# Opening weights in 512-byte rows on one queue, and a first wave by pairs of rows

## The chip, the cores and the metric

The kernel runs on one core of one Trainium2 chip. The metric is the device time of one execution in microseconds (us). Times come from plain executions; the views come from one profiled execution, whose own time is given beside its span.

## The reference

A layer norm over the last axis without scale and shift, a matrix product with a bias and a tanh-approximated gelu, and a second matrix product with a bias. All inputs and the output are bf16.

```python
B, S, D, F = 1, 2048, 1024, 3584

def reference(x, w1, b1, w2, b2):
    y = _layernorm(x, axis=-1)                               # eps 1e-5
    h = _gelu(jnp.einsum("bsd,df->bsf", y, w1) + b1)          # w1: D x F
    return jnp.einsum("bsf,fd->bsd", h, w2) + b2              # w2: F x D
```

## The kernel before

**Tiling.** The 2,048 tokens are four blocks of 512 (`TB`), each of four tiles of 128 tokens. The contraction over D = 1,024 has eight blocks of 128, called dt (`DT`). The F = 3,584 hidden columns are 28 row blocks of 128, called r (`FT`). The first product computes, for row r, a [128 hidden x 512 tokens] piece in one PSUM bank from eight matmuls, one for each dt; ScalarE applies the gelu with the bias and writes `hT_sb`. The second product takes 28 matmuls for each [128 tokens x 512 columns] piece of the output; VectorE adds b2 and SyncE stores. All weights stay in SBUF.

**How the order is made.** Each engine has its own program, a list filled by the Python code and emitted at the end. The order within an engine is the order in which the lines are appended; a wait sits in front of the operation that has it, and everything behind it on that engine waits too. Signals between engines are semaphores; each DMA has a semaphore of its own, which counts sixteen parts, one from each of the sixteen DMA engines.

**The opening, which the change touches.** The first block can't wait for its layer norm, so its four tiles go three ways.

- Tiles 0 and 1 (`RAW`) are multiplied raw, without mean and scale. `pe_T(0, ...)` and `pe_T(1, ...)` transpose them on TensorE, ScalarE copies them to `yT_sb` (line 353). Statistics go on the side, and the result is repaired in PSUM: `ops_fix` adds the mean times the column sum of the weights and multiplies by the scale (lines 512 and 515), then comes the gelu. For the later rows (r of 7 and up) the transposed tiles are centred in place, `ops_centre` (line 505), and only the scale is applied in PSUM (line 420). The centring overwrites what the first wave reads, so it waits for the wave's last matmul (`wave01`).
- Tiles 2 and 3 are normalised by VectorE (`op_stats` line 250, `op_aggr` line 260 with a power on GpSimd at line 257, `ops_norm` line 264) and then transposed on TensorE; these transposes are called T2 and T3.
- The first seven rows (`R_WAVE`) run as waves over seven PSUM banks, cell by cell, all at line 394. A cell is one matmul: row r, contraction block dt. The first wave, over tiles 0 and 1, has 56 cells of 258 columns (two of them hold ones, which give the column sums). Then tile 2 has 56 cells of 128 columns, in the order halves of dt, rows, dt in the half. Then tile 3 has 56 cells, row by row. From row 7 on, `mm1_row` takes all four tiles at once (line 381).

The first wave runs dt by dt: all seven rows for dt 0, then all seven for dt 1. Its weights come in the same way, one transfer for each dt with the columns of all seven rows (896 columns, 1,792 bytes per row of w1). T2 stands ahead of dt 6 (`T2_BEFORE`), T3 after 14 cells of tile 2's wave (`T3_AT`).

**The queues.** SyncE (SP) issues x0, x1, w0, w2, x2, w4, w5, x3, w6, w7 and then the rest: the other columns of w1 (640, 1,024 and 1,024 wide, all eight dt in one transfer), x for the second block, w2 in four parts, b2, the rest of x. ScalarE (ACT) issues b1, w1 and w3, where w1 and w3 are here the transfers of dt 1 and dt 3. All are made at line 187.

**VectorE's order in the opening** (line 521): the statistics of tiles 0 and 1; the bias operations `ops_b1` (lines 490 and 493), which turn b1 into a column for each row; the statistics of tile 2; the first half of `ops_row_turn` (line 479), which turns the statistics of the raw tiles into rows; the norm of tile 2; the statistics of tile 3; the second half of the turn; the norm of tile 3; `ops_row_spread` (line 484), which copies those rows to all partitions; the two centrings; then the fixes.

Of the kernel before, what the change touches and what calls it, by code (L numbers as in the profile page):

```python
# [12 lines left out]
P = 128  # L13
TB = 512
TPB = TB // P
# [5 lines left out]
RAW = (0, 1)  # L21
# [2 lines left out]
GROUPS_0 = (0, 4, 8)  # L24
GROUPS_1 = (0, 8)
HALVES = (0, 4, 8)
T2_BEFORE = 6
T3_AT = 14
W1_COLS = (640, 1024, 1024)
N_W2_CHUNKS = 4  # L30
SP_FIRST_LOADS = ("x0", "x1", "w0", "w2", "x2", "w4", "w5", "x3", "w6", "w7")
ACT_FIRST_LOADS = ("b1", "w1", "w3")
SLOT_0 = (1, 2, 3, 0)
N_ONES = 2

# [56 lines left out]
def bass_standalone__mixer_channel_mlp__prompt_kernel(  # L92
# [13 lines left out]
    DT = D // P  # L106
# [7 lines left out]
    R = R_WAVE  # L114
    assert R == NB1 + NB2 and R < FT
    assert NB1 + NB2 + 1 <= 8 and NB2 == 2
    assert all(c[-1] == DT for c in (GROUPS_0, GROUPS_1, HALVES))
    assert T2_BEFORE < DT and TPB == 4 and RAW == (0, 1)

    w1_chunks = [(j, j + 1, 0, R * P) for j in range(DT)]  # L120
    c0 = R * P
    for wdt in W1_COLS:
        w1_chunks.append((0, DT, c0, c0 + wdt))
        c0 += wdt
# [17 lines left out]
    with ExitStack() as es:  # L142
# [67 lines left out]
        def issue(item):  # L210
            if item == "b1":
                dma(b1r_sb[0:FT, :], b1.rearrange("(t p) -> t p", p=P), "b1", F * 2, waits=["b1z"])
            elif item[0] == "x":
                load_x_tile(int(item[1:]))
            elif item[0] == "w" and int(item[1:]) < len(w1_chunks):
                load_w1(int(item[1:]))

        act.op(lambda e: e.preload_act_table(ACT.Gelu_apprx_tanh))
        dma_q[0] = act
        for item in ACT_FIRST_LOADS:  # L220
            issue(item)
        dma_q[0] = sp
        for item in SP_FIRST_LOADS:
            issue(item)
# [18 lines left out]
        for i in range(NT):  # L243
            n = 6 * parts(i)
# [3 lines left out]
        def op_stats(i, h):  # L248
            pw = D // parts(i)
            return (lambda e, i=i, h=h, pw=pw: e.bn_stats(st_sb[i][:, 6 * h:6 * (h + 1)],  # L250
                                                          x_sb[:, i, h * pw:(h + 1) * pw]),
                    [x_ev[i][h if len(x_ev[i]) == parts(i) else 0]], f"st{i}_{h}", 0.03 + pw * 0.0012)

        def op_aggr(i):
            mv = stat_r[:, i, 0:2] if i in RAW else mv_sb[:, i, :]
            dst = stat_r[:, i, 2:3] if i in RAW else rstd_sb[:, i:i + 1]
            pool.op(lambda e, i=i, dst=dst, mv=mv: e.tensor_tensor(out=dst, in0=mv[:, 1:2], in1=nhalf[:, i:i + 1],  # L257
                                                                   op=ALU.pow),
                    waits=[f"mv{i}", "nhalf"], sig=f"rstd{i}")
            return (lambda e, i=i, mv=mv: e.bn_aggr(mv, st_sb[i][:, :]),  # L260
                    [f"st{i}_{parts(i) - 1}", f"eps{i}"], f"mv{i}", 0.33)
# [9 lines left out]
        def ops_norm(i):  # L271
            cuts = (0, DT)
            y_ev[i] = []
            res = []
            for k, (j0, j1) in enumerate(zip(cuts[:-1], cuts[1:])):
                res.append(op_norm(i, j0 * P, j1 * P, f"y{i}_{k}"))
                y_ev[i] += [f"y{i}_{k}"] * (j1 - j0)
            return res
# [84 lines left out]
        def new_unit():  # L363
            u = unit_n[0]
            unit_n[0] += 1
            bank = first_ring[u] if u < len(first_ring) else ("1", (u - len(first_ring)) % NB1)
            waits = [bank_gelu[bank]] if bank in bank_gelu else []
            name = f"{bank[0]}_{bank[1]}"
            if not waits and name in bank_read:
                waits.append(bank_read[name])  # L370
            return bank, waits
# [16 lines left out]
        def pe_wave(r, dt, tiles, bank, waits, sig):  # L388
            n0 = slot(tiles[0]) * P - (N_ONES if tiles[0] == 0 else 0)
            n1 = (slot(tiles[-1]) + 1) * P  # L390
            w = list(waits) + [f"w1c{w1_chunk_of(r, dt)}"] + [yT_ev[t][dt] for t in tiles]
            if tiles[0] == 0:
                w.append("onecols")
            pe.op(lambda e: e.matmul(  # L394
                unit_bank(bank)[:, n0:n1], lhsT=w1_sb[:, dt, r * P:(r + 1) * P], rhs=yT_sb[:, 0, dt, n0:n1],
                start=(dt == 0 and tiles[0] in (0, 3)), stop=(dt == DT - 1), skip_group_check=True),
                waits=w, sig=sig)
            pe_t[0] += _mm_us(n1 - n0)
            if sig:
                est[sig] = pe_t[0]  # L400
# [73 lines left out]
        def ops_row_turn():  # L474
            res = []
            for tq in range(4):
                src = flat[32 * tq:32 * (tq + 1), :, :].to_broadcast([32, 4, 32])
                dst = row_r[0:32, :, 32 * tq:32 * (tq + 1)]
                res.append((lambda e, src=src, dst=dst: e.transpose(out=dst, in_=src), ["rstd0", "rstd1"],
                            ("row_q" if tq == 3 else None), 0.31))  # L480
            return res

        def ops_row_spread():
            return [(lambda e, q=q: e.tensor_copy(out=row_r[32 * q:32 * (q + 1), :, :], in_=row_r[0:32, :, :]),
                     ["row_q"], ("row_r" if q == 3 else None), 0.35) for q in range(1, 4)]

        def ops_b1():
            res = []
            for q in range(4):
                res.append((lambda e, q=q: e.transpose(out=b1t_sb[32 * q:32 * (q + 1), :],  # L490
                                                       in_=b1r_sb[:, 32 * q:32 * (q + 1)]),
                            ["b1", "b1z"], ("b1t" if q == 3 else None), 0.2))
            res.append((lambda e: e.tensor_copy(out=b1_sb[:, :], in_=b1t_sb[:, 0:FT]), ["b1t"], "b1c", 0.18))
            return res
# [5 lines left out]
        def ops_centre():  # L500
            res = []
            for t in RAW:
                xt = yT_sb[:, 0, :, slot(t) * P:(slot(t) + 1) * P]
                m = row_r[:, 2 * t, :].unsqueeze(1).to_broadcast([P, DT, P])
                res.append((lambda e, xt=xt, m=m: e.tensor_tensor(out=xt, in0=xt, in1=m, op=ALU.subtract),  # L505
                            ["row_r", "wave01"], f"ctr{t}", 1.23))
            return res
# [10 lines left out]
        st = {i: [op_stats(i, 0), op_stats(i, 1), op_aggr(i)] for i in range(TPB)}  # L518
        nm = {i: ops_norm(i) for i in (2, 3)}
        turn = ops_row_turn()  # L520
        seq = st[0][:2] + st[1][:2] + [st[0][2], st[1][2]] + ops_b1()
        seq += st[2] + turn[:2] + nm[2] + st[3] + turn[2:] + nm[3] + ops_row_spread() + ops_centre()
        for o in seq:
            dve_put(o)

# [3 lines left out]
        wave = [new_unit() for _ in range(R)]  # L529
        opened = set()  # L530

        def wave_cell(r, dt, tiles, sig=None):
            waits = [] if r in opened else wave[r][1]
            opened.add(r)
            pe_wave(r, dt, tiles, wave[r][0], waits, sig)

        early = [r for r in range(R) if not wave[r][1]] + sorted((r for r in range(R) if wave[r][1]),
                                                                 key=lambda r: wave[r][1])
        for dt in range(DT):
            if dt == T2_BEFORE:  # L540
                pe_T(2, GROUPS_1, ("t",))
            for k, r in enumerate(early):
                wave_cell(r, dt, RAW, "wave01" if dt == DT - 1 and k == R - 1 else None)
        n = 0
        for j0, j1 in zip(HALVES[:-1], HALVES[1:]):
            for r in range(R):
                for dt in range(j0, j1):
                    if n == T3_AT:
                        pe_T(3, GROUPS_1, ("t",))
# [25 lines left out]
        for b in range(NB):  # L575
# [11 lines left out]
            for st in range(TPB):  # L587
                for dh in range(DH):
                    c0, c1 = dh * NCH, (dh + 1) * NCH
# [72 lines left out]
```

## Time and profile before

| | before |
|---|---|
| runs | 399.11, 399.95, 398.2 us |
| median | 399.11 us |
| profiled execution, its own time | 399.24 us |
| its span | 397.8 us |
| PE busy | 392.0 us (99%) |
| DVE busy | 155.1 us (39%) |
| ACT busy | 81.0 us (20%) |
| weights of the opening (224 KB each) from SP, issue to landing | 6.5 us median of six |
| x tiles of 256 KB, issue to landing | 4.9 us median of four |
| granted TensorE clock | 1.0 |

PE is TensorE, PEld its weight loads, DVE is VectorE, ACT is ScalarE, POOL is GpSimd and SP is SyncE. A busy PE in this table means that matmuls were in flight. Times inside the execution count from the start of the span. The chain of waits is the work that ended last, followed back from the last instruction to what released it.

### The profile page before, as it was taken

The numbers are of one execution on the slowest core, as the hardware profiler recorded it, in microseconds if no ns is written. First come the engines' busy times: TensorE is split into PE (matmuls) and PEld (weight loads), VectorE is DVE, ScalarE is ACT, GpSimd is POOL, SyncE is SP. The second block draws the span as 40 slices with busy tenths as digits, with TensorE's granted clock in tenths as the row PEclk, the third lists the DMA queues.
The fourth block names the chain that finished last, engine by engine and source line by source line (L and its number), as shares of the span: only waits on it lengthen the run. The fifth ranks groups of instructions, "written<-read, shape, count | busy, mean of one in ns | idle before, by whom it ended". The sixth has DMA issues, their size and how long they took to land.

```text
span 397.8 us, 4722 instructions
## 1 busy us (share of the span) xinstructions
PE 392.0 (99%) x2017; PEld 190.9 (48%) x2052; DVE 155.1 (39%) x338; ACT 81.0 (20%) x121; POOL 10.6 (3%) x56
## 2 busy tenths in 40 slices
PE   7999999999999999999999999999999999999998
PEld 7954444444444444444444444444444444444447
DVE  4968898989999004988100000001100000001011
ACT  2163430000034432000024334100003334400000
POOL 2101000010001000000000000000000000000000
PEclk9999999999999999999999999999999999999999
DMA  7999930000000000000000000000000000000001
GB/s 254 384 386 387 387 134 15 26 25 17 26 1 2 0 0 2 26 14 28 26 15 0 0 2 0 7 21 26 13 28 13 2 0 0 2 13 26 15 26 28
DMA packets 15326, 23.64 MB, mean 59 GB/s; under 512 B 1482, under 2 KB 7498, under 8 KB 15306
## 3 DMA queue, kind: packets, MB, share of 16 engines
q1 hardware_dynamic: 14976, 22.88, 16.1%
q10 hardware_dynamic: 330, 0.47, 0.4%
q8 instruction: 16, 0.26, 0.3%
q14 instruction: 4, 0.03, 0.0%
HBM read 19.14 MB, written 4.19 MB: 59 GB/s over the span
## 4 chain that ended last, share of the span: by engine, by line
PE 97%; DMA 1%; issue 1%; SPq 0%; DVE 0%
PE ps L446 48%; PE ps L381 45%; PE ps L394 3%; DMA w_sb<-in_w_dram 1%; PE ps_t L337 0%; SPq L187 0%; DVE o_sb L457 0%
## 5 line engine op out<-in xcount | busy, mean ns | idle before, releaser
L446 PE MATMUL ps<-w_sb,hT_sb 128*128 128x512 bf16 (+1 forms) x964 | 193.4, 360 | 0.8
L381 PE MATMUL ps<-yT_sb,w_sb 128*128 128x512 bf16 x821 | 180.8, 379 | 1.0
L446 PEld LDWEIGHTS ps<-w_sb,hT_sb 128*128 128x128 bf16 x980 | 91.3, 98 | 102.7
L381 PEld LDWEIGHTS ps<-yT_sb,w_sb 128*128 128x128 bf16 x840 | 82.2, 98 | 98.9
L404 ACT ACTIVATE hT_sb<-ps,b_sb 128x512 bf16<-128x512 f32 x112 | 76.7, 687 | 253.2 <-PE ps L381 231.8
L457 DVE TENSOR_TENSOR o_sb<-ps,b_sb 128x512 bf16<-128x512 f32 (+1 forms) x35 | 22.6, 646 | 198.9 <-PE ps L446 198.9
L307 DVE STREAM_TRANSPOSE yT_sb<-x_sb 32x256 bf16<-32x256 bf16 x192 | 83.7, 436 | 26.4 <-PE ps L381 23.3
L250 DVE BATCH_NORM_STATS2 st_sb<-x_sb 128x6 f32<-128x512 bf16 x32 | 20.9, 670 | 8.6 <-DMA x_sb<-in_x_dram 8.5
L394 PE MATMUL ps<-yT_sb,w_sb 128*128 128x128 bf16 (+1 forms) x168 | 12.9, 237 | 1.4 <-DMA w_sb<-in_w_dram 1.4
L394 PEld LDWEIGHTS ps<-yT_sb,w_sb 128*128 128x128 bf16 x168 | 11.7, 98 | 2.3 <-DMA w_sb<-in_w_dram 1.6
L257 POOL TENSOR_TENSOR rstd_sb<-mv_sb,nhalf 128x1 f32<-128x1 f32 x14 | 7.7, 548 | 115.3 <-DVE mv_sb L260 115.3
L420 DVE TENSOR_TENSOR ps<-ps,row_r 128x256 f32<-128x256 f32 x21 | 8.8, 426 | 3.9 <-PE ps L381 3.7
L264 DVE TENSOR_SCALAR x_sb<-x_sb,mv_sb,rstd_sb 128x1024 bf16<-128x1024 bf16 x14 | 7.6, 544 | 2.5 <-POOL rstd_sb L257 1.8
L468 PE MATMUL ps<-const-bfloat16-1.0 128*128 128x128 bf16 x32 | 3.8, 310 | 0.8 <-PEq L647 0.8
L353 ACT COPY yT_sb<-ps_t 128x512 int32<-128x512 int32 (+1 forms) x3 | 1.5, 514 | 11.4 <-PE ps_t L337 11.4
L468 PEld LDWEIGHTS ps<-const-bfloat16-1.0 128*128 128x128 bf16 x32 | 3.4, 144 | 0.8 <-issue 0.8
L512 DVE SCALAR_TENSOR_TENSOR ps<-row_r,ncs,ps 128x256 f32<-128x256 f32 x7 | 3.3, 478 | 0.0
L260 DVE BATCH_NORM_AGGREGATE mv_sb<-st_sb 128x2 f32<-128x15 f32 x14 | 3.1, 221 | 0.4
L515 DVE TENSOR_TENSOR ps<-ps,row_r 128x256 f32<-128x256 f32 x7 | 3.0, 432 | 0.2
L505 DVE TENSOR_TENSOR yT_sb<-yT_sb,row_r 128x1024 bf16<-128x1024 bf16 x2 | 2.4, 1222 | 0.0
L337 PE MATMUL ps_t<-ident,x_sb 128*128 128x128 bf16 x20 | 1.8, 236 | 0.0
L337 PE MATMUL ps<-ident,x_sb 128*128 128x128 bf16 x12 | 1.5, 311 | 0.0
(21 smaller groups left out, 13.4 us busy)
## 6 DMA issues: line engine op xcount, KB each, us to landing
w_sb<-in_w_dram SPq DMA_DIRECT2D x4, 1792.0 KB, 18.9
w_sb<-in_w_dram SPq DMA_DIRECT2D x2, 2048.0 KB, 17.3
out_dram<-o_sb SPq DMA_DIRECT2D x31, 128.0 KB, 1.7
x_sb<-in_x_dram SPq DMA_DIRECT2D x3, 1024.0 KB, 14.0
w_sb<-in_w_dram SPq DMA_DIRECT2D x6, 224.0 KB, 6.5
w_sb<-in_w_dram SPq DMA_DIRECT2D x1, 1280.0 KB, 10.3
x_sb<-in_x_dram SPq DMA_DIRECT2D x4, 256.0 KB, 4.9
w_sb<-in_w_dram ACTq DMA_DIRECT2D x2, 224.0 KB, 6.2
```

The costliest lines, as they stand in the source:

```text
L250: return (lambda e, i=i, h=h, pw=pw: e.bn_stats(st_sb[i][:, 6 * h:6 * (h + 1)], x_sb[:, i, h * pw:(h + 1) * pw]), [x_ev[i][h if len(x_ev[i ...
L257: pool.op(lambda e, i=i, dst=dst, mv=mv: e.tensor_tensor(out=dst, in0=mv[:, 1:2], in1=nhalf[:, i:i + 1], op=ALU.pow), waits=[f"mv{i}", "nh ...
L264: return (lambda e, i=i, c0=c0, c1=c1: e.tensor_scalar(out=x_sb[:, i, c0:c1], in0=x_sb[:, i, c0:c1], scalar1=mv_sb[:, i, 0:1], scalar2=rst ...
L307: res.append((lambda e, src=src, dst=dst: e.transpose(out=dst, in_=src), waits, (f"tr{i}" if lastop else None), 0.47))
L337: pe.op(lambda e, i=i, j=j, o=off, bap=bank_of[bname]: e.transpose(out=bap[:, o:o + P], in_=x_sb[:, i, j * P:(j + 1) * P], identity=ident[ ...
L381: pe.op(lambda e, b=b, r=r, dt=dt, bank=bank: e.matmul(unit_bank(bank)[:, 0:TB], lhsT=w1_sb[:, dt, r * P:(r + 1) * P], rhs=yT_sb[:, b % 2, ...
L394: pe.op(lambda e: e.matmul(unit_bank(bank)[:, n0:n1], lhsT=w1_sb[:, dt, r * P:(r + 1) * P], rhs=yT_sb[:, 0, dt, n0:n1], start=(dt == 0 and ...
L404: act.op(lambda e, r=r, n0=n0, n1=n1, bank=bank: e.activation(out=hT_sb[:, r, n0:n1], in_=unit_bank(bank)[:, n0:n1], func=ACT.Gelu_apprx_tanh,
L420: crit.append((est[sig], (lambda e, reg=reg: e.tensor_tensor(out=reg, in0=reg, in1=row_b(1), op=ALU.mult), [sig, "row_r"], ready, 0.45), 0))
L446: pe.op(lambda e, sl=sl, ft=ft, c0=c0, c1=c1, bank=bank: e.matmul(ps_2[:, bank, 0:c1 - c0], lhsT=hT_sb[:, ft, sl * P:(sl + 1) * P], rhs=w2 ...
L457: crit.append((est[sig], (lambda e, ob=ob, c0=c0, c1=c1, bank=bank: e.tensor_tensor(out=o_sb[:, ob, c0:c1], in0=ps_2[:, bank, 0:c1 - c0], ...
L468: pe.op(lambda e: e.matmul(ps_1[:, 0, 0:P], lhsT=ones, rhs=ones, start=True, stop=True))
```

## The change

The opening weights are cut another way. Instead of eight transfers of one contraction block each, with 896 columns (128 rows of 1,792 bytes), there are eight of four contraction blocks each, with 256 columns (512 rows of 512 bytes): the columns of two rows r, dt 0 to 3 in one transfer and dt 4 to 7 in the next. They hold eight rows r (1,024 columns), so that the next transfer has 512 columns in place of 640. All eight go on SyncE's queue, in order, with x2 after the first two and x3 after the sixth; ScalarE issues b1 alone.

The first wave follows: by pairs of rows (0,1), (2,3), (4,5) and then row 6, in each pair the first half of dt for its rows, then the second half. T2 now stands ahead of cell 40, which is the second half of the pair (4,5); T3 stands after 28 cells of tile 2's wave, which are all rows' first halves.

VectorE's order changes as well. The bias operations move from ahead of tile 2's statistics to behind the row spread; tile 3's statistics move behind them; the first centring moves ahead of tile 3's norm.

```diff
@@ -24,12 +24,15 @@
 GROUPS_0 = (0, 4, 8)
 GROUPS_1 = (0, 8)
 HALVES = (0, 4, 8)
-T2_BEFORE = 6
-T3_AT = 14
-W1_COLS = (640, 1024, 1024)
+PAIRS = ((0, 1), (2, 3), (4, 5), (6,))
+T2_AT = 40
+T3_AT = 28
+W1_EARLY = 4
+W1_EARLY_COLS = 256
+W1_COLS = (512, 1024, 1024)
 N_W2_CHUNKS = 4
-SP_FIRST_LOADS = ("x0", "x1", "w0", "w2", "x2", "w4", "w5", "x3", "w6", "w7")
-ACT_FIRST_LOADS = ("b1", "w1", "w3")
+SP_FIRST_LOADS = ("x0", "x1", "w0", "w1", "x2", "w2", "w3", "w4", "w5", "x3", "w6", "w7")
+ACT_FIRST_LOADS = ("b1",)
 SLOT_0 = (1, 2, 3, 0)
 N_ONES = 2
 
@@ -115,10 +118,11 @@
     assert R == NB1 + NB2 and R < FT
     assert NB1 + NB2 + 1 <= 8 and NB2 == 2
     assert all(c[-1] == DT for c in (GROUPS_0, GROUPS_1, HALVES))
-    assert T2_BEFORE < DT and TPB == 4 and RAW == (0, 1)
-
-    w1_chunks = [(j, j + 1, 0, R * P) for j in range(DT)]
-    c0 = R * P
+    assert TPB == 4 and RAW == (0, 1) and sum(PAIRS, ()) == tuple(range(R))
+
+    w1_chunks = [(j0, j1, k * W1_EARLY_COLS, (k + 1) * W1_EARLY_COLS) for k in range(W1_EARLY)
+                 for j0, j1 in zip(HALVES[:-1], HALVES[1:])]
+    c0 = W1_EARLY * W1_EARLY_COLS
     for wdt in W1_COLS:
         w1_chunks.append((0, DT, c0, c0 + wdt))
         c0 += wdt
@@ -518,8 +522,9 @@
         st = {i: [op_stats(i, 0), op_stats(i, 1), op_aggr(i)] for i in range(TPB)}
         nm = {i: ops_norm(i) for i in (2, 3)}
         turn = ops_row_turn()
-        seq = st[0][:2] + st[1][:2] + [st[0][2], st[1][2]] + ops_b1()
-        seq += st[2] + turn[:2] + nm[2] + st[3] + turn[2:] + nm[3] + ops_row_spread() + ops_centre()
+        ctr = ops_centre()
+        seq = st[0][:2] + st[1][:2] + [st[0][2], st[1][2]] + st[2] + turn[:2] + nm[2] + turn[2:] + ops_row_spread()
+        seq += ops_b1() + st[3] + ctr[:1] + nm[3] + ctr[1:]
         for o in seq:
             dve_put(o)
 
@@ -534,13 +539,12 @@
             opened.add(r)
             pe_wave(r, dt, tiles, wave[r][0], waits, sig)
 
-        early = [r for r in range(R) if not wave[r][1]] + sorted((r for r in range(R) if wave[r][1]),
-                                                                 key=lambda r: wave[r][1])
-        for dt in range(DT):
-            if dt == T2_BEFORE:
+        cells = [(r, dt) for rows in PAIRS for j0, j1 in zip(HALVES[:-1], HALVES[1:])
+                 for r in rows for dt in range(j0, j1)]
+        for n, (r, dt) in enumerate(cells):
+            if n == T2_AT:
                 pe_T(2, GROUPS_1, ("t",))
-            for k, r in enumerate(early):
-                wave_cell(r, dt, RAW, "wave01" if dt == DT - 1 and k == R - 1 else None)
+            wave_cell(r, dt, RAW, "wave01" if n == len(cells) - 1 else None)
         n = 0
         for j0, j1 in zip(HALVES[:-1], HALVES[1:]):
             for r in range(R):
```

## The prediction

> **What bounds the kernel now.** I read the chain of waits first, in order of time. Columns: start us, length us, what; x counts instructions.
>
> ```profile
> by line: PE ps L446 48.5%; PE ps L381 45.3%; PE ps L394 3.2%; DMA w_sb<-in_w_dram 1.5%; issue 0.5%; PE ps_t L337 0.2%; SPq L187 0.2%; DVE o_sb L457 0.1%
> ...
> 1.70 5.85 DMA w_sb<-in_w_dram
> 7.54 0.05 issue
> 7.59 4.79 PE ps L394 x42
> 12.38 0.48 PE ps_t L337 x8
> 12.86 2.32 PE ps L394 x28
> 15.19 0.45 PE ps_t L337 x8
> 15.63 5.47 PE ps L394 x98
> 21.10 0.05 issue
> 21.16 10.74 PE ps L381 x49
> ```
>
> From 7.59 on TensorE never waits until the end, and from 21.10 on nothing that the diff touches runs. So the whole question is by how much the moment 21.10 (row 7's first matmul, line 381) moves. Two prices come from here: a wave matmul over two tiles is 4.79/42 = 0.114 us, one over one tile 5.47/98 = 0.0558 us. The 0.48 and 0.45 are the transposes of tile 2 (T2) and tile 3 (T3).
>
> Next I read the stretches of the opening (length, busy us of PE, PEld, DVE, ACT, POOL, granted clock, DMA share, GB/s) and the DMA view of two stretches with one packet size each.
>
> ```profile
> 3.60:5.20 1.60, 1.60 (x17) 1.60 (x17) 1.60 (x3) 0.87 (x3) 0.00 (x0) 1.00 0.79 242
> 10.00:12.00 2.00, 2.00 (x20) 1.77 (x19) 1.76 (x6) 0.00 (x0) 0.55 (x1) 1.00 1.05 387
> ```
> ```profile
> DMA packets 876, 1.14 MB, mean 381 GB/s; under 512 B 19, under 2 KB 854, under 8 KB 876
> ...
> q1 hardware_dynamic: 876, 1.14, 106.3%
> ```
> ```profile
> q1 hardware_dynamic: 570, 1.14, 103.4%
> ```
>
> The last two are 11:14 and 24:27. Between 3.6 and 5.2 the 16 DMA engines are busy to 0.79, later to 1.05. The landing events of the trace say where that goes: of the 16 parts of the first weight transfer (issued 1.70) twelve land by 5.93 and four at 7.34 to 7.54, and those four engines stay about 2 us behind to the end of the opening. PE starts when the late four arrive.
>
> The third view is VectorE's timeline (start, length), since it makes tile 3's normalised rows.
>
> ```profile
> 6.14 0.79 DVE L490 STREAM_TRANSPOSE b1t_sb<-b1r_sb 32x32 bf16<-32x32 bf16 x4
> 6.96 0.18 DVE L493 CAST b_sb<-b1t_sb 128x28 f32<-128x28 bf16 x1
> ...
> 9.43 1.29 DVE L250 BATCH_NORM_STATS2 st_sb<-x_sb 128x6 f32<-128x512 bf16 x2 [2.29 <-DMA x_sb<-in_x_dram]
> ...
> 12.10 1.28 DVE L250 BATCH_NORM_STATS2 st_sb<-x_sb 128x6 f32<-128x512 bf16 x2
> ...
> 13.67 0.62 DVE L479 STREAM_TRANSPOSE row_r<-stat_r 32x128 f32<-32x128 f32 x2
> ...
> 14.32 0.55 DVE L264 TENSOR_SCALAR x_sb<-x_sb,mv_sb,rstd_sb 128x1024 bf16<-128x1024 bf16 x1
> 14.89 1.28 DVE L484 COPY row_r<-row_r 32x512 f32<-32x512 f32 x3
> ```
>
> VectorE waits for x2 (landed 9.41) and from then on runs without a gap. The norm of tile 3 ends at 14.87, and T3 starts at 14.97: no slack there to give away.
>
> **Transfers.** Removed: eight loads of 128 rows of 1,792 bytes, two of them issued by ScalarE (0.37 and 0.44 us of its queue at 2.00, ahead of a copy that waits for PE until 4.22: nothing is won there). Added: eight loads of 512 rows of 512 bytes, all from SyncE. x2 is still SyncE's fifth issue (2.65 us); x3 goes from eighth to tenth, w6 and w7 behind it, at some 0.47 us an issue: issued by 6 us, landed after 12, so no issue decides.
>
> Price of a packet: 11:14 gives 1.063 x 48 / 876 = 58 ns for 1,301 bytes on average, 24:27 gives 1.034 x 48 / 570 = 87 ns for 2,005 bytes. The line through both gives 26 ns at 512 bytes; the 256-byte packets of b1 take 18 ns and 4-byte ones 9, which gives 27. No 512-byte packet is in this trace, so the bounds are 18 ns and, far above, the 55 ns of 1,280 bytes. I take 27, next to both lines. An engine moves 32 packets per load: 32 x 27 ns = 0.86 us (bounds 0.58 and 1.76), against 0.60 now (w4 landed 10.01, w5 10.61). An x tile takes 0.69 (w5 to x3, 11.30).
>
> The Trainium skill (DMA: Bandwidth & Descriptors, Specifications) puts the smallest transfer at line rate at 512 bytes. By that rule these rows run at the 387 GB/s of 10:12, 0.68 us a load, and the sum below would come to 400.6 us.
>
> Where does the late engine's work start? Now w7 lands at 12.58; less eight loads at 0.60 and x2, x3 at 0.69 it is 6.40, though x1 had landed whole at 4.17: 2.2 us are lost. I keep 6.40, because nothing in the change removes what stopped those engines that I can point to; the other bound is 4.17.
>
> - w0: 6.40 + 0.86 = 7.26 (now 7.54).
> - x2: 6.40 + 2 x 0.86 + 0.69 = 8.81 (now 9.41).
> - w7: 6.40 + 8 x 0.86 + 2 x 0.69 = 14.66 (now 12.58).
>
> **The wave.** Pairs of rows eat a load in eight cells, 0.91 us, so PE is fed load by load and the last four cells wait for w7: the wave over tiles 0 and 1 ends at 14.66 + 4 x 0.114 = 15.12. T2 (cell 40) falls in these gaps: its norm is ready at 8.81 + 2.8 = 11.6, its place comes at 12.3. Now the wave ends about 14.5. Four matmuls in a row to one bank cost nothing: line 394's one-tile wave does that at 0.0558.
>
> **VectorE's order.** The bias operations leave the idle time at 6.14 (cover gone: 1.00 us on the path) and go, with the three copies of line 484, ahead of x3's statistics; the first centring (line 505, which waits for the wave's end) goes ahead of tile 3's norm. That is the added wait: behind it stand the norm, the second centring and the fixes, and PE's T3 waits for the norm, with all that is behind T3. From x2's landing D:
>
> - x2 statistics, two transposes, norm: 12.10 - 9.41 = 2.69
> - two transposes 0.62, copies 14.89 to 16.21 1.32, bias 1.00: D + 5.63
> - x3 statistics and aggregate (12.10 to 13.67) 1.57: D + 7.20 = 16.01. x3 landed at 13.0, and the wave's end reaches VectorE at 15.12 + 0.2 (a drain of 0.16 and the semaphore), so VectorE itself is last.
> - centring 2.36/2 = 1.18, norm 0.55, to PE 0.05: T3 at D + 8.98 = 17.79
>
> PE gets to T3 28 cells after the wave, 15.12 + 1.56 = 16.68, and waits 1.1 us. Then T3 0.45, the other 28 cells 1.56, tile 3's 56 cells 3.13: row 7 starts at 17.79 + 5.14 = 22.93. **Sum: 22.93 - 21.10 = +1.8 us.** In general it starts at the later of D + 14.1 and wave end + 7.1 (0.2 + 1.18 + 0.55 + 0.05 + 5.14).
>
> Afterwards all is covered: the first fix follows T3 by 2.7 us, its gelu 1.7 later, before row 7 (5.1 after T3) takes that bank. w8 now brings 512 columns in 1,024-byte rows (64 x 46 ns = 2.9 us), so lands near 17.6, for row 8 at 24.7. Everything after it is about 1.3 us late; the last w2 part lands near 50 and is wanted at 57.2.
>
> The profiled execution took 399.24 us for a span of 397.8, 0.13 over the median. 399.24 + 1.83 - 0.13 = 400.94: I write **401.0**.
>
> **Rivals.**
>
> 1. *The lateness goes with the second queue.* For it: the idle engines of 3.6:5.2 come just as both queues carry weights. Against it: x alone, on one queue, has some long packets too. Then the loads start at 4.17, D = 4.17 + 1.73 + 0.69 = 6.59, row 7 at 20.7: -0.4 us, 398.7. Half the lateness gives 399.9. The floor for any transfer is the warm-up's end 6.21 + 56 x 0.114 + 0.45 + 7.1 = 20.2, so -0.9 us is all that can be won.
> The Trainium skill (DMA: Bandwidth & Descriptors, Issuing engines are not separate DMA queues) holds that a second queue saves issue time alone; by that this rival is wrong. The late stretch, 242 GB/s with both queues, neither proves nor refutes it.
> 2. *The 512-byte rows cost more than the line says (the slower side).* Rows 7,168 bytes apart, four regions at once: if such a packet takes 40 ns, a load takes 1.28, w7 lands at 18.0, the wave ends at 18.5 and row 7 starts at 25.6: +4.5, 403.6; at 55 ns 407.4. The last load decides over VectorE from 6 x load > 5.85, 0.975 us a load or 30.5 ns a packet: close to my 27. For it: the first weight packets of now, with one region each, already stalled. Against it: packets of 1,280 bytes at the same pitch run at 381 GB/s.
> 3. *It doesn't do what it says*: VectorE's order is harmless because the wave is late anyway. Then 15.12 + 7.1 = 22.2, +1.1, 400.2; the first pair still starts only 0.3 us sooner, since w0 hangs on the late engines.
>
> **Chances.** Forecast 0.42 (own range 400.3 to 402.2), rival 1 0.18 with half lateness 0.10, rival 2 0.25, rival 3 0.05. Range 398.9 to 404.2: it leaves out the lower half of rival 1 and the worst third of rival 2. 0.5% is 2.0 us, about what a measurement of this kernel tells from no change: the limits are 397.1 and 401.1. Faster needs twice the floor: 0.03. Slower holds rival 2 and more than half of the forecast, whose neglected gaps all go one way: 0.52. Within: 0.45.
>
> **What would show it.** w0 landing near 7.3 and the wave's first matmul right behind; first-wave pieces broken by waits for w_sb; w7 near 14.7; line 505's first instruction ahead of tile 3's norm; an idle of 1.1 us ahead of T3 put down to DVE; row 7 at 22.9. Wrong if 512-byte packets take over 30 ns, if w0 lands whole before 6.2, or if PE doesn't wait at T3.

## The result, and the profile after

The changed kernel takes 400.85 us (median of 9 runs, 400.15 to 401.49), the kernel before 398.6 beside it (9 runs, 398.2 to 399.95). The ratio is 1.0053, with a 95% interval of 1.004 to 1.0066: slower by 2.1 us, where +1.8 and 401.0 were forecast.

The two profiled executions show less than that, 400.15 against 399.24. They aren't typical: 400.15 is the fastest of the nine runs of the changed kernel, 399.24 lies in the upper part of the runs of before. Spans 398.6 and 397.8 differ by 0.8, and row 7's start accounts for it: 21.90 against 21.16.

The chain of waits of the changed kernel, in order of time (start us, length us, what):

```profile
2.70 4.44 DMA x_sb<-in_x_dram
...
12.96 1.20 DVE st_sb L254 x2
14.49 1.42 POOL rstd_sb L261
15.93 0.56 DVE x_sb L268
16.54 0.62 PE ps_t L341 x8
17.16 4.69 PE ps L398 x84
21.90 10.74 PE ps L385 x49
```

Before, this stretch was a transfer of weights and then TensorE alone. Now it runs from x2's transfer (landed at 7.14) through VectorE and GpSimd to T3, and only then TensorE takes over. The waits of TensorE up to 30 us (who waited for whom: us in total, times, longest):

```profile
PE ps_t L341 <- DVE x_sb L268: 1.1, 1, 1.1
PE ps L398 <- DMA w_sb<-in_w_dram: 1.1, 3, 0.5
```

The wave does begin sooner, at 5.65 in place of 7.59. The three waits for weights of the second line stand ahead of the cells at 5.65, 8.09 and 13.24, and T3 waits 1.1 us for tile 3's norm. VectorE and GpSimd ahead of T3 (start, length):

```profile
10.59 1.28 DVE L488 COPY row_r<-row_r 32x512 f32<-32x512 f32 x3
...
11.90 0.85 DVE L494 STREAM_TRANSPOSE b1t_sb<-b1r_sb 32x32 bf16<-32x32 bf16 x4
...
12.88 1.28 DVE L254 BATCH_NORM_STATS2 st_sb<-x_sb 128x6 f32<-128x512 bf16 x2
...
14.33 1.16 DVE L509 TENSOR_TENSOR yT_sb<-yT_sb,row_r 128x1024 bf16<-128x1024 bf16 x1
14.49 1.41 POOL L261 TENSOR_TENSOR rstd_sb<-mv_sb,nhalf 128x1 f32<-128x1 f32 x1 [5.16 <-DVE mv_sb L264]
15.93 0.55 DVE L268 TENSOR_SCALAR x_sb<-x_sb,mv_sb,rstd_sb 128x1024 bf16<-128x1024 bf16 x1 [0.44 <-POOL rstd_sb L261]
```

x3 had landed at 11.41; its statistics start at 12.88, behind the bias operations. Tile 3's norm waits for the centring and then 0.44 us more for GpSimd's power, which takes 1.41 us here and took 0.55 before.

### The profile page after: what moved, and what is told of

It is laid out like the page before. It is cut to its first block, busy times and chain, and to the rows that moved or that the text cites. A ratio compares the mean times of both kernels' runs of the same rounds, so it can differ in the third digit from the quotient of the medians.

```text
span 398.6 us, 4722 instructions
## 1 busy us (share of the span) xinstructions
PE 391.8 (98%) x2017; PEld 189.7 (48%) x2052; DVE 155.5 (39%) x338; ACT 80.7 (20%) x121; POOL 11.4 (3%) x56
## 4 chain that ended last, share of the span: by engine, by line
PE 95%; DVE 2%; DMA 1%; issue 1%; POOL 0%; SPq 0%
PE ps L450 48%; PE ps L385 45%; PE ps L398 1%; DMA x_sb<-in_x_dram 1%; POOL rstd_sb L261 0%; DVE st_sb L254 0%; SPq L191 0%; DVE row_r L488 0%; DVE x_sb L268 0%; DVE b1t_sb L494 0%; PE ps_t L341 0%; DVE row_r L483 0%; DVE mv_sb L264 0%; DVE o_sb L461 0%; DVE b_sb L497 0%
## 5 line engine op out<-in xcount | busy, mean ns | idle before, releaser
L261 POOL TENSOR_TENSOR rstd_sb<-mv_sb,nhalf 128x1 f32<-128x1 f32 x14 | 8.5, 609 | 115.1 <-DVE mv_sb L264 115.1
L341 PEld LDWEIGHTS ps_t<-ident,x_sb 128*128 128x128 bf16 x20 | 1.3, 104 | 1.6 <-DVE x_sb L268 1.3
```

## The experiments

All times are ratios to runs of the kernel before on the same chip. "x2 landed" and "row 7" are read in each run's own profile.

**1. The changed kernel with VectorE's old order.**

```diff
-        seq = ... + st[2] + turn[:2] + nm[2] + turn[2:] + ops_row_spread()
-        seq += ops_b1() + st[3] + ctr[:1] + nm[3] + ctr[1:]
+        seq = ... + ops_b1()
+        seq += st[2] + turn[:2] + nm[2] + st[3] + turn[2:] + nm[3] + ops_row_spread() + ctr
```

> The changed kernel with VectorE's old order (bias early, tile 3's statistics and norm ahead of the copies and of both centrings). Theory 1, VectorE's order sets row 7's start (x2's landing + 14.7 us in the profile of the changed kernel, the wave's end + 6.7 without it): T3 no longer waits, row 7 starts about 1.5 us sooner, near 20.4 in a profile with the same landings; time 399.3 us, ratio to before 1.002 (1.000 to 1.003). Theory 2, the last weight load sets it: T3 and tile 3's wave are held by the wave in any case, at most 0.4 us is won, ratio 1.0045 to 1.006 as for the changed kernel.

399.62 us, 1.0007 (0.9989 to 1.0025). Its profile (399.72) has x2 landed at 8.21, later than that of the changed kernel, and yet row 7 starts sooner. Counted from x2, row 7 comes after 13.29 us (21.50 - 8.21) in place of 14.76 (21.90 - 7.14): 1.47 us are won, where 1.5 were expected. Its chain of waits:

```profile
8.60 5.55 DMA w_sb<-in_w_dram
14.14 0.05 issue
14.19 2.18 PE ps L398 x32
16.36 0.45 PE ps_t L341 x8
16.81 4.69 PE ps L398 x84
21.50 2.59 PE ps L385 x12
```

T3 follows the wave without a wait, and the last 512-byte load (landed 14.14) sets the time. VectorE's order is worth 0.46% (1.0053 to 1.0007, and the two intervals don't touch), nearly the whole loss; theory 2 of that run falls.

**2 and 3. One half of it each:** the norm ahead of the first centring, and the bias operations back in the idle time.

```diff
 # run 2
-        seq += ops_b1() + st[3] + ctr[:1] + nm[3] + ctr[1:]
+        seq += ops_b1() + st[3] + nm[3] + ctr
 # run 3
-        seq = st[0][:2] + st[1][:2] + [st[0][2], st[1][2]] + st[2] + ...
+        seq = st[0][:2] + st[1][:2] + [st[0][2], st[1][2]] + ops_b1() + st[2] + ...
-        seq += ops_b1() + st[3] + ctr[:1] + nm[3] + ctr[1:]
+        seq += st[3] + ctr[:1] + nm[3] + ctr[1:]
```

> The changed kernel with one swap: tile 3's norm ahead of the first centring, bias still late. Theory 1: the norm no longer stands behind 1.2 us of centring, and the power on GpSimd, which took 1.41 us beside the centring in the profile of the changed kernel, takes 0.55 again; the norm still waits for that power. T3 starts near 15.7 in place of 16.54, row 7 0.8 us sooner; ratio to before 1.0035. Theory 2: no change, 1.0053.

> The changed kernel with the bias operations back in the idle time ahead of tile 2's statistics, first centring still ahead of the norm. Theory 1: VectorE's chain is 1.0 us shorter; then the centring waits for the wave's end and T3 starts near 15.7, row 7 0.8 us sooner; ratio to before 1.0035. The power on GpSimd then ends before the centring begins and takes 0.55 us. Theory 2: no change, 1.0053.

Run 2: 1.0016 (1.0005 to 1.0027). Run 3: 1.0027 (1.0016 to 1.0037). T3 waits less than the 1.1 us of the changed kernel in both (run 2, then run 3; the wait is in brackets):

```profile
16.49 0.62 PE L341 MATMUL ps_t<-ident,x_sb 128*128 128x128 bf16 x8 [0.27 <-DVE x_sb L268]
```
```profile
15.87 0.62 PE L341 MATMUL ps_t<-ident,x_sb 128*128 128x128 bf16 x8 [0.22 <-DVE x_sb L268]
```

Since x2 lands at another time in each profile (7.14 changed, 7.95 run 2, 7.35 run 3), T3 has to be counted from there: 9.40 us after x2 in the changed kernel, 16.49 - 7.95 = 8.54 in run 2, 15.87 - 7.35 = 8.52 in run 3. In run 3 the chain no longer comes from x2 but from the last weight load (landed 13.43) through the wave's end and the centring, as expected; counted from that load T3 comes after 2.44 us, in place of 3.35 in the changed kernel. Each half gives T3 back 0.9 us, a little more than the 0.8 expected, and the power takes 0.55 us in both. In time run 3 is near its 1.0035, and run 2 misses it: it gives back 0.37%, or 1.5 us (0.8 to 2.2 by the two intervals), where T3's 0.9 us would be 0.23%. The two halves needn't add up to run 1, since each of them alone already ends the slow power.

**4. VectorE's new order alone, in the kernel before.** The diff is that of run 1 the other way round.

> The kernel before with VectorE's new order alone: loads, queues, wave and the places of T2 and T3 as before. Theory 1: T3, which started at 15.19, waits until x2's landing + 9.0 to 9.4, that is 18.4 to 18.8 by the landing 9.41 of the profile before; row 7 starts 3.2 to 3.6 us later; ratio to before 1.008 to 1.009. Theory 2 (VectorE's order costs nothing, the loads do): ratio 1.000 to 1.001.

1.0138 (1.0118 to 1.0158), 5.5 us: well over the expectation. T3 comes at 18.73, 9.40 after x2's landing (9.33), inside the range. What was not expected comes behind it. The chain, and the stretches of 2 us (length, busy PE, PEld, DVE, ACT, POOL, granted clock, DMA share, GB/s):

```profile
16.68 1.42 POOL rstd_sb L257
18.10 0.03 issue
18.12 0.56 DVE x_sb L264
18.68 0.04 issue
18.73 0.62 PE ps_t L337 x8
19.35 7.10 PE ps L394 x98
```
```profile
16.00:18.00 2.00, 0.00 (x0) 0.00 (x0) 1.65 (x3) 0.00 (x0) 1.32 (x1) 1.00 1.05 386
18.00:20.00 2.00, 1.27 (x18) 1.28 (x19) 1.68 (x2) 0.59 (x1) 0.09 (x1) 0.86 1.05 387
20.00:22.00 2.00, 2.00 (x22) 2.00 (x20) 0.00 (x0) 0.00 (x0) 0.00 (x0) 0.50 1.05 388
22.00:24.00 2.00, 2.00 (x32) 2.00 (x30) 0.20 (x1) 0.35 (x2) 0.00 (x0) 0.79 1.05 387
```

The wait of 3.62 us was followed by a granted clock of 0.50, from 19.43 to 22.85 by the clock's own record: 98 one-tile cells take 7.10 us where before they took 5.47. T3 thus starts 3.54 us later than in the profile before (18.73 against 15.19), and 1.6 us more are lost behind it. All five executions of this run have a mean clock under 1.0 (0.992 to 0.996). The changed kernel's wait of 1.1 us cost no clock; every run of it has 1.0.

**5. One queue, with the loads and the wave of before.**

```diff
-SP_FIRST_LOADS = ("x0", "x1", "w0", "w2", "x2", "w4", "w5", "x3", "w6", "w7")
-ACT_FIRST_LOADS = ("b1", "w1", "w3")
+SP_FIRST_LOADS = ("x0", "x1", "w0", "w1", "x2", "w2", "w3", "w4", "w5", "x3", "w6", "w7")
+ACT_FIRST_LOADS = ("b1",)
```

> The kernel before with all eight of its 1,792-byte loads on SyncE's queue, in the order of the change (x2 after two loads, x3 after six); wave, VectorE's order and all else as before. Theory 1, the second queue makes four engines late (profiles so far: the first load's sixteen parts land within 2.6 to 3.1 us of each other with two queues, within 0.6 to 1.8 us with one): the first load lands at 5.2 to 6.3, the first wave starts at about 6.0 in place of 7.3 to 7.6 and never waits, row 7 starts near 19.6 to 20.2; time 0.5 to 1.2 us under the kernel before, ratio 0.997 to 0.999. Theory 2, the lateness belongs to the start of the weights whatever the queue: the first load lands at 6.5 to 7.5, ratio 0.999 to 1.001.

398.35 us, 0.9971 (0.9959 to 0.9983): faster than both kernels. Its chain:

```profile
3.13 5.15 DMA w_sb<-in_w_dram
8.28 0.05 issue
8.33 3.25 PE ps L394 x28
11.58 0.45 PE ps_t L337 x8
12.03 2.32 PE ps L394 x28
14.35 0.45 PE ps_t L337 x8
14.80 5.47 PE ps L394 x98
20.27 0.05 issue
20.32 3.83 PE ps L381 x17
```

Row 7 starts 0.84 us sooner than in the profile before. The time came out as theory 1 had it, the landing between the theories: the first load's last part lands at 6.49, and its sixteen parts still spread over 2.1 us. The wave starts at 6.54 and pauses once more for a load (ahead of 8.33), so row 7 comes at 20.32 and not by 20.2. So the second queue isn't all of the lateness.

**6. Two queues in the changed kernel**, the opposite.

```diff
-SP_FIRST_LOADS = ("x0", "x1", "w0", "w1", "x2", "w2", "w3", "w4", "w5", "x3", "w6", "w7")
-ACT_FIRST_LOADS = ("b1",)
+SP_FIRST_LOADS = ("x0", "x1", "w0", "w2", "x2", "w4", "w5", "x3", "w6", "w7")
+ACT_FIRST_LOADS = ("b1", "w1", "w3")
```

> The changed kernel with two of its 512-byte loads (the second and the fourth) issued by ScalarE, as the kernel before issued two of its own; all else as changed. Theory 1: the first load's parts spread over 2.5 us or more again, x2 lands near 8.8 to 9.3 in place of 7.1 to 8.2, T3 starts 9.4 later, row 7 near 23.5 to 24; ratio to before 1.009 to 1.011. Theory 2: as the changed kernel, 1.005 to 1.006.

1.0102 (1.0074 to 1.0129), as theory 1 had it. The first load lands at 7.84 (parts spread over 3.0 us), x2 at 10.52, later than expected, T3 comes at 19.92, once more 9.40 after x2. The one queue of the change is thus a gain. But this run changes the order as well: on one queue x2 stands behind two weight loads, here it stands behind two of SyncE's while ScalarE's two share the engines. The median of x2's sixteen parts lands 1.7 us later than in the changed kernel (8.29 against 6.58), about two loads of 0.86; only the rest of the 3.4 us is lateness of the last engines. The first load has the same place in both kernels, and there the queue shows by itself: its last part lands at 7.30 to 7.84 in the three profiles with two queues, and at 5.18 to 6.58 in the six that have one queue and this load third. In TensorE's timeline T3 waits 2.6 us, and the stretch behind it has the clock at 0.50 again:

```profile
19.92 1.03 PE L341 MATMUL ps_t<-ident,x_sb 128*128 128x128 bf16 x8 [2.62 <-DVE x_sb L268]
```
```profile
20.00:22.00 2.00, 2.00 (x20) 2.00 (x21) 1.00 (x1) 0.58 (x1) 0.00 (x0) 0.50 1.05 386
```

This execution is the slowest of six; three of them, this one included, have a mean clock of 0.992 to 0.996 (403.95 to 405.05 us), three have 1.0 (402.05 to 402.81). So a part of the ratio is lost clock, which the expectation didn't have: the three at full clock average 402.5, 0.9% over the 399.05 of the kernel before at full clock.

**7. Rows of 1,024 bytes, with VectorE's old order:** two contraction blocks by 512 columns in a load, the wave by rows 0 to 3 and 4 to 6.

```diff
-PAIRS = ((0, 1), (2, 3), (4, 5), (6,))
-W1_EARLY = 4
-W1_EARLY_COLS = 256
+PAIRS = ((0, 1, 2, 3), (4, 5, 6))
+QUARTERS = (0, 2, 4, 6, 8)
 ...
+W1_EARLY = 2
+W1_EARLY_COLS = 512
 ...   # QUARTERS for HALVES in w1_chunks and cells; VectorE's order as in run 1
```

> The changed kernel with VectorE's old order and eight 256 KB loads of two contraction blocks by 512 columns (1,024-byte rows); the first wave runs by rows 0 to 3 and 4 to 6, two contraction blocks at a time, so that a load still feeds eight cells (six in the second half). Beside the same with 512-byte rows (399.62 us, 1.0007), where the last early load landed at 14.14 and set T3 and row 7. If the packets' cost sets the end there: a load takes 16 x 51 ns = 0.82 in place of 0.90 (51 ns is what 1,024-byte packets took in the profile of the changed kernel), the last one lands 0.6 us sooner, row 7 too; ratio 0.999 to 1.0. If it doesn't (something else holds the opening): 1.0007 as there.

398.74 us, 0.9985 (0.997 to 1.0). In its profile the last loads land 0.75 us apart, against 0.80 to 0.90 with 512-byte rows in run 1, and the last one at 12.62 in place of 14.14. That is more than the 0.6 us expected, and on the last engines most of it is not the packets: the first load is whole 1.40 us sooner too (5.18 against 6.58). On the typical engine the packets show: the median part of the first load lands at the same time (4.88 and 4.94), that of the last one 1.0 us sooner (11.88 and 12.87). So a load of longer rows is cheaper, but how much of the time that is stays open: run 7's interval overlaps that of run 1 (0.9989 to 1.0025), and the wave's order changed with the rows. The difference, 0.22%, is less than the 0.46% of VectorE's order, but the intervals don't separate the two.

**8 and 9. The first load ahead of x1, and ahead of both x tiles**, on the kernel of run 5.

```diff
-SP_FIRST_LOADS = ("x0", "x1", "w0", "w1", ...)
+SP_FIRST_LOADS = ("x0", "w0", "x1", "w1", ...)      # run 8
+SP_FIRST_LOADS = ("w0", "x0", "x1", "w1", ...)      # run 9
```

> The one-queue kernel with 1,792-byte loads (0.9971, first load landed at 6.49, wave started at 6.54) with its first load moved ahead of x1. If the wave's start is what is left of the opening and the load's lateness moves with the load: it lands about 0.7 us sooner, at 5.5 to 5.9; x1 lands 0.6 later, at 4.8 to 5.2, its transposes end near 5.7 and their copies near 6.3, so the wave starts near 6.2 to 6.4: 0.1 to 0.4 us sooner, ratio 0.9962 to 0.997. If the lateness holds a fixed moment of the clock, whichever transfer it meets (the four late parts at about 6 to 6.5): no gain or a loss, 0.997 to 0.999.

> The same with the first load ahead of x0 and x1. If the lateness belongs to the first reads of w1, it now begins 1.3 us sooner and delays x0 and x1 on the late engines: x0 lands at 4 to 5.5, the transposes wait, the wave starts at 6.5 to 7.5 and VectorE's statistics of tiles 0 and 1 slip; ratio 0.997 to 1.0005. If it belongs to a fixed moment or to the queue: the load lands near 3.6, x0 near 4.2, x1 near 4.9, the wave starts near 6.1; ratio 0.996 to 0.997.

Run 8: 0.9994 (0.9971 to 1.0018). Run 9: 1.0005 (0.9985 to 1.0024). The gain of run 5 doesn't show in either, though run 8's interval still reaches down to it, and both show where the lateness sits. (Their profiled executions are slow ones of their kind: 400.7 us for a median of 399.63, and 401.52, the slowest of twelve.) In run 9 the first weight load lands whole by 3.36, with 0.5 us between its parts; x0 lands by 4.22; then x1, now third, has twelve parts by 6.41 and the last at 6.80, after a first at 4.58. In run 8 x1 is third as well, and its parts spread from 4.55 to 6.35. So the lateness doesn't belong to the weights: in these two runs it meets x1, which is third, between about 3.6 and 7 us. The expectation for run 9's time was wrong on that account, since x1's transposes then wait. TensorE also reaches its full clock late: the clock's record begins at 11.68 in run 9 and at 4.04 to 6.17 in the five other profiles that have one, and run 9's chain has the first 42 cells at 6.17 us long, against 4.79 before; the cells start 0.215 us apart until 11.65 and 0.11 from then on. Run 8 has cells 0.215 apart too, until 9.91. That the idle time ahead of the wave (for x1, 1.8 us in run 8 and 1.5 in run 9) is what delays the clock was not tested.

```profile
1.69 5.12 DMA x_sb<-in_x_dram
6.80 0.05 issue
6.85 1.04 PE ps L337 x8
7.89 0.75 PE ps L468 x7
8.63 6.17 PE ps L394 x42
```

Whether the third place or the moment decides wasn't tried, nor what makes these engines wait. Run 7 speaks against the place alone: the parts of its third transfer lie within 0.42 us, no wider than those of the first two transfers in any profile (0.2 to 0.6), and the spread jumps to 1.5 only at its seventh, between 7.5 and 9.0 us. One candidate was never taken away: ScalarE's transfer of b1, whose parts land between 3.4 and 4.4 us in every profile (but for one at 2.1).

## Why the prediction came out as it did

The time, its sign and the chief mechanism were right. One term of the sum was mis-sized, and two small ones that were missing made up part of it, so that the nearness of the number is in part luck.

- **What bounds the kernel**: right. Only row 7's start moved: 0.74 us in the two profiles, with spans 0.8 apart. (The prediction's 21.10 is where the wave ends; row 7's first matmul stands at 21.16. Its 22.93 is such an end too, so the difference holds.)
- **Price of a packet**: right. 32 x 27 ns = 0.86 us a load was forecast; loads that follow one another land 0.86 to 0.92 us apart (the first two 0.75). From 8 to 9.4 us of the changed kernel, where 795 of 802 packets are under 2 KB, 16 engines x 1.4 us / 802 is 27.9 ns a packet. Rival 2, the dear packets, falls. So does the line rate for 512-byte rows that the Trainium skill states (DMA: Bandwidth & Descriptors, Specifications): the stretch runs at 292 GB/s, against 387 with the long rows of before.

```profile
DMA packets 802, 0.41 MB, mean 292 GB/s; under 512 B 24, under 2 KB 795, under 8 KB 802
```

- **"I keep 6.40"**, the start of the late engines' work: the mis-sized term. With one queue the first load landed at 5.61 and x2 at 7.14 in the changed kernel's profile, not 7.26 and 8.81; runs 1 to 3, with the same loads, have x2 at 8.21, 7.95 and 7.35. The 2.2 us of lateness that the trace showed with two queues became 0.5 to 1.6 (x2 without any would be at 6.6). The prediction's own sign of being wrong, a first load whole before 6.2, came true, in runs 2 and 3 as well (6.06 and 5.40). Rival 1 was therefore right in part: its half lateness puts x2 at 7.7, and the mean of these four landings is 7.66. Runs 5 and 6 agree that the second queue had its share. The rule that it was weighed against (Trainium skill, DMA: Bandwidth & Descriptors, Issuing engines are not separate DMA queues) doesn't settle this opening: as that section has it, one set of engines serves both queues, but the first load then shares them with the second queue's, and one queue in place of two is worth 0.3% in run 5, where x2 also comes ahead of two more loads.
- **VectorE's chain**: right in its steps, short by 0.42 us. T3 was to come 8.98 us after x2; it came 9.40 after in three profiles (changed kernel, runs 4 and 6). The missing piece is GpSimd's power, which the first centring now overlaps: 1.41 us in place of 0.55, so that the norm waits 0.44 us behind the centring. Another 0.17 came from T3 itself, 0.62 us when TensorE had waited, 0.45 when not.
- **The wait**: 1.1 us forecast, 1.1 measured, by two errors that cancel: TensorE was at T3 at 15.42 and not 16.68, and T3 could start at 16.54 and not 17.79. That there is a wait, and for what, was right; its exact size is luck. Rival 3, VectorE's order being harmless, falls with run 1.
- **The sum** for the profiled execution: 1.67 us too much for x2, 0.42 + 0.17 too little behind it, so 21.85 and not 22.93, which is where the trace has it. That execution is the fastest of nine, and others may have x2 later. With the four landings of x2 (7.14 to 8.21) and the 14.76 us from x2 to row 7, the changed kernel would be 0.7 to 1.8 us behind the profile before, 1.3 on average; that profile's execution is itself 0.6 us above the median of 398.6. This estimate makes 1.9 of the 2.1 us. Profiles of slower executions of the changed kernel weren't taken.

In ratios: one queue gives 0.29% (run 5), the 512-byte rows with the pairs cost 0.36% (run 5 to run 1), VectorE's order 0.46% (run 1 to the change). Each of these is uncertain by 0.1 to 0.2%, and they hold for this order of steps: in the kernel before, where T3 was due 5.8 us after x2 and not 8.3, and where the clock fell, VectorE's order alone cost 1.38% (run 4). An earlier start was won, and more was given back behind it.

## What to carry to other kernels

When a wave is made to start sooner, follow every operand that is still due behind it: here the weights came sooner and tile 3's norm didn't, since work that had cost nothing in an idle stretch was put on its path. Judge an order on VectorE together with the engine that its result passes through, for the power on GpSimd slowed as soon as a two-input operation ran beside it. And count a transfer's landing by its last engine, in several profiles, before a time is built on it.

## What was not expected of the hardware

- GpSimd's [128 x 1] power takes 0.55 us alone and 1.40 to 1.42 us when the 1.16 us centring (two inputs in SBUF) has begun 0.16 us ahead of it, in all three profiles that have this order; it ends 0.41 us after the centring. In run 3, where the power starts first, it takes 0.55. The Trainium skill (SBUF — State Buffer, Who interferes with whom) says that such an operation of VectorE and one of GpSimd that reads SBUF share one read path, and that the second to start is blocked until the first is done; these rows agree with that.
- The clock fell to half for 3.41 us after waits of 3.62 us (run 4) and of only 2.62 us (run 6), and not after 1.4 us (the profile before) or 1.1 us (the changed kernel). Both falls came 13.65 us after the full clock was granted. The Trainium skill (TensorE: Matmul & The Clock Gate, What's actually happening and Why this matters for your kernels) tells of a free-running window of 3.4 us and advises against gaps over about 3; the wait of 2.62 us shows that a shorter one can be enough. It isn't the same in every execution: half of run 6's keep the clock, and of the 71 executions of the kernel before that stand beside the nine runs, 11 have a mean clock of 0.996 and take 400.39 to 401.84 us, where the others average 399.1. None of those was profiled.
- In the opening some of the 16 DMA engines fall behind from about 3.6 us on, in nine of the eleven profiles at the third transfer, weights or x: its parts land over 2.6 to 3.1 us in the three with two queues and over 1.0 to 2.2 in six with one, against 0.2 to 0.6 in the first two transfers. In runs 3 and 7 the third is like the first two (0.6 and 0.4), and the spread grows behind it.
